# Fused attention and gated feed-forward, one core: how the first batch's keys and queries are loaded, cast and waited for

## The chip, the cores and the metric

The kernel runs on one core of one Trainium2 chip. The metric is device time in microseconds (us) of one execution. The core has a TensorE (PE, with its weight loads listed apart as PEld), a VectorE (DVE), a ScalarE (ACT), a GpSimd (POOL) and a SyncE (SP). SP, ACT and POOL each have a queue from which DMA transfers are issued. In the profile, L185 means line 185 of the kernel.

## The reference

Attention with a squared Relu in place of the softmax, in 8 batches of 12 heads of 448 positions by 64, followed by a gated feed-forward layer on the 3584 rows of 768:

```python
def _attn_ref(q, k, v):
    S = q.shape[2]
    scale = 1.0 / np.sqrt(q.shape[-1])
    scores = scale * np.matmul(q, k.transpose(0, 1, 3, 2))
    attn = np.maximum(scores, 0.0) ** 2 / S
    return np.matmul(attn, v)

def _moe_ref(x, w_gate, w_val, w_out):      # w_gate, w_val: 768 x 1536
    gate = np.maximum(x @ w_gate, 0.0)
    return (gate * (x @ w_val)) @ w_out
```

Inputs and output are float32; the kernel computes in bfloat16 with float32 sums.

## The kernel before

**Layout.** Keys, queries and values of a batch stand in SBUF as `kn`, `qn` and `vn`, `[128, 12, 4, 64]` in bf16: 64 partitions hold four positions each ("lo", positions 0 to 255) and 64 hold three ("hi", 256 to 447). There are two buffers of each. Loading a range of heads of one tensor takes two DMAs, lo and hi (`load_nat`). Pool's queue does this and casts from float32 to bf16 on the way. SP's and ACT's queues cannot cast, so `load_first` brings the first heads of batch 0 as float32 into `kr` and `qr` (tiles that are used for other things much later) and an engine casts them into `kn` and `qn`.

**Order of the loads.** `load_first(2)` brings heads 0 and 1 by SP (lo) and ACT (hi). Then Pool makes the identity matrix and issues, in this order: keys and queries of heads 2 and 3, of heads 4 to 7, of heads 8 to 11 (twelve DMAs), the values of batch 0, the first two chunks of the gate and value weights, batch 1's keys and queries, and the other weights, with `wo` (two halves) last. At most eight of Pool's DMAs are under way at once, in turn.

**Staging.** `first_batch` does batch 0's attention without other work beside it. Heads go in pairs: `transposes` turns a pair's keys and queries by TensorE (matmuls against `ident`, L178) into a PSUM bank, and VectorE copies them out as `kq_sb` (L180). There are 21 tiles of scores, taken in trios: tile 0 to 2 need pair 0, tile 3 to 5 pairs 0 and 1, tile 6 pair 1, tiles 7 and 8 pair 2, and so on. After each trio's scores TensorE transposes the next pair and does a few matmuls on zeros (`idle_matmuls`, on `blank`, two per pair of halves). A tile's scores go to one of three PSUM buffers; ScalarE applies Relu (L185), VectorE squares (L189). From the sixth trio on (tiles `u0` to `u2`, then `w0` to `w2`), `values(qd, c)` multiplies the squared scores with the values, and `cast` brings the result from PSUM into `xT`, the feed-forward layer's input. VectorE does five of these casts (L391) and ScalarE one (L428). Everything is held in program order on each engine (`pin`), so an instruction that waits holds all that follow on its engine.

After that come the units of the feed-forward layer (`gv_unit`: gate and value products, L64 from `mm`; `out_unit`: products with `wo`), mixed with the attention of the next batches. `wo` is first used at about 62 us.

**Lines that the change touches:** `load_first` (L95 to L108), the calls after it in the kernel's body, and `first_batch` with `values`, `cast` and the first `idle_matmuls`. Before, the table of ScalarE's activation functions is loaded (ACT_TABLE_LOAD) ahead of its first activation, the cast of the queries on L108.

Of the kernel before, what the change touches and what calls it, by code (L numbers as in the profile page):

```python
# [10 lines left out]
BF16 = mybir.dt.bfloat16  # L11
AF = mybir.ActivationFunctionType
# [4 lines left out]
def kernel(  # L17
# [15 lines left out]
    nc = tc.nc  # L33

    B, H, S, D = q.shape
# [18 lines left out]
    rpool = ctx.enter_context(tc.tile_pool(name="rpool", bufs=4))  # L54
# [5 lines left out]
    def pin(ins):  # L60
        return tc.keep_in_program_order(ins)
# [4 lines left out]
    def mm2(o, l, r, start, stop):  # L66

        for c in range(2):
            p = slice(c * 64, c * 64 + 64)
            mm(o[p], l[:, p], r, start, stop)  # L70

    NB = 2
    blank = const.tile([128, S], BF16, name="blank")
    pin(nc.vector.memset(blank, 0.0))
    kn_b = [const.tile([128, H, 4, D], BF16, name=f"kn{i}") for i in range(NB)]
    qn_b = [const.tile([128, H, 4, D], BF16, name=f"qn{i}") for i in range(NB)]
# [8 lines left out]
    kr = const.tile([128, 4, d_model], BF16, name="kr")  # L85
    qr = const.tile([128, 4, d_model], BF16, name="qr")

    def make_ident():
        pin(nc.gpsimd.affine_select(out=ident, in_=ident, compare_op=ALU.not_equal, fill=1.0, base=0,
                                    pattern=[[-1, 128]], channel_multiplier=1))  # L90

    def dma_in(o, i):
        pin(nc.gpsimd.dma_start(out=o, in_=i))  # L93

    def load_first(h1):  # L95

        staged = []
        for grp, src in ((kr, k), (qr, q)):
            st = grp.rearrange("p i m -> p (i m)")[:, 0:h1 * 8 * D].bitcast(FP32)
            st = st.rearrange("p (h i d) -> p h i d", i=4, d=D)  # L100
            pin(nc.gpsimd.memset(st[64:128, :, 3, :], 0.0))
            lo = src[0, 0:h1, 0:256, :].rearrange("h (j i) d -> j h i d", i=4)
            hi = src[0, 0:h1, 256:448, :].rearrange("h (j i) d -> j h i d", i=3)
            pin(nc.sync.dma_start(out=st[0:64], in_=lo))
            pin(nc.scalar.dma_start(out=st[64:128, :, 0:3, :], in_=hi))
            staged.append(st)
        pin(nc.vector.tensor_copy(kn_b[0][:, 0:h1], staged[0]))
        pin(nc.scalar.activation(qn_b[0][:, 0:h1], staged[1], AF.Copy))  # L108

    def load_nat(dst, src, b, h0, h1):  # L110
        lo = src[b, h0:h1, 0:256, :].rearrange("h (j i) d -> j h i d", i=4)
        hi = src[b, h0:h1, 256:448, :].rearrange("h (j i) d -> j h i d", i=3)
        dma_in(dst[0:64, h0:h1, :, :], lo)
        dma_in(dst[64:128, h0:h1, 0:3, :], hi)

    def load_qk(b, h0=0, h1=H):
        load_nat(kn_b[b % NB], k, b, h0, h1)
        load_nat(qn_b[b % NB], q, b, h0, h1)

    def load_v(b):  # L120
        load_nat(v_b[b % NB], v, b, 0, H)

    def low_values(b):

        t = v_b[b % NB].rearrange("p (q s h) i d -> p q s h i d", s=2, h=2)
        pin(nc.vector.tensor_copy(t[64:128, :, 1, :, 3, :], t[0:64, :, 1, :, 3, :]))
# [64 lines left out]
    def relu2(src, dst, n):  # L191
        square_part(dst, relu_part(src, n))
# [31 lines left out]
    def av_pair(b, qd, c, attn, ps):  # L224

        p = HALVES[c][1]
        for h2, o in HALVES:
            mm(ps[o, :S], v_b[b % NB][p, 4 * qd + 2 * c + h2, 3, :], attn[p, 6 + h2, :], True, False)
        for i in range(3):
            for h2, o in HALVES:  # L230
                mm(ps[o, :S], v_b[b % NB][:, 4 * qd + 2 * c + h2, i, :], attn[:, 8 * c + 2 * i + h2, :], False, i == 2)

    def bank_tile():
        return psum.tile([128, 512], FP32, name="xT_ps", tag="acc", bufs=2)

    def idle_matmuls(ps, n):

        for _ in range(n):
            mm2(ps[:, :S], blank[:, 0:128], blank, True, True)
# [86 lines left out]
    def gap():  # L326
# [4 lines left out]
        flush()  # L331
        share[2] = i + 1

    load_first(2)
    make_ident()
    load_qk(0, 2, 4)
    load_qk(0, 4, 8)
    load_qk(0, 8, H)
    load_v(0)
    load_gv(0)  # L340
    load_gv(1)
# [14 lines left out]
    def transpose_pair(b, hp, bank=None):  # L356
        kqs[b, hp] = operands(b, hp, bank)

    def attn_of(b, qd):
        if (b, qd) not in attns:  # L360
            attns[b, qd] = atpool.tile([128, 14, S], BF16, name="attn")
        return attns[b, qd]

    def burst(b, tiles):

        todo, begun = [], None
        for qd, kind, c, i in tiles:
            attn = attn_of(b, qd)
            if kind == "pair":
                todo.append(scores(kqs[b, 2 * qd + c], i, attn, 8 * c + 2 * i))  # L370
            elif kind == "last":
                todo.append(scores_last((kqs[b, 2 * qd], kqs[b, 2 * qd + 1]), attn))
            else:
                ps = sc_tile()
                banks = [ps[:, c, :S] for c in range(2)]
                av_last(b, qd, attn, banks)
                begun = (qd, banks, ps[:, :, :S])
        return todo, begun

    def first_batch():  # L380

        def tile_of(n, i):
            return burst(0, [tiles_first[3 * n + i]])[0][0]

        def values(qd, c, on_act=False):
            ps, x = bank_tile(), xT_of[0][:, 2 * qd + c, :]
            av_pair(0, qd, c, attn_of(0, qd), ps)
            return x, ps[:, :S]

        def cast(x, ps):  # L390
            pin(nc.vector.tensor_copy(x, ps))  # L391

        bank = bank_tile()
        idle_matmuls(bank, 14)
        transpose_pair(0, 0, bank)
        bank = bank_tile()
        idle_matmuls(bank, 4)
        for n in range(5):
            t = [tile_of(n, i) for i in range(3)]
            if n == 4:  # L400
                low_values(0)
            transpose_pair(0, n + 1, bank)
            if n < 4:
                bank = bank_tile()
                idle_matmuls(bank, 2)
                for u in t:
                    relu2(*u)
        relu2(*t[0])
        relu2(*t[1])
        u0 = tile_of(5, 0)  # L410
        cast(*values(0, 0))
        relu2(*t[2])
        u1 = tile_of(5, 1)
        cast(*values(0, 1))
        u2 = tile_of(5, 2)
        relu2(*u0)
        relu2(*u1)
        w0 = tile_of(6, 0)
        cast(*values(1, 0))
        relu2(*u2)  # L420
        w1 = tile_of(6, 1)
        cast(*values(1, 1))
        w2 = tile_of(6, 2)
        relu2(*w0)
        relu2(*w1)
        x, ps = values(2, 0)
        relu2(*w2)
        pin(nc.scalar.activation(x, ps, AF.Copy))  # L428
        cast(*values(2, 1))


# [43 lines left out]
    for b in range(B):  # L475
        xT_of[b] = xpool.tile([128, KD, S], BF16, name="xT")
        if b == 0:
            first_batch()
        else:
            batch(b)  # L480
        if b + 1 < B:
            ffn.extend(ffn_units(b))
            if b == 0:
                for _ in range(7):
                    ffn.pop(0)()
                for hp in range(2):
                    midway.append(lambda hp=hp: transpose_pair(1, hp))
                ffn.pop(0)()
# [34 lines left out]
```

## Time and profile before

| | |
|---|---|
| median of 3 runs | 436.48 us (435.64 to 436.99) |
| the profiled execution | 436.3 us, of which 434.5 us are the profile's span |
| TensorE busy | 425.1 us, 98% of the span |
| ScalarE, VectorE, GpSimd busy | 217.6, 210.3 and 50.5 us |
| HBM read, written | 47.19 and 11.01 MB |
| Pool's DMA queue (software_dynamic) | 45152 packets, 23.47 MB |

The span runs from the first instruction to the last; the other 1.8 us of the execution lie around it. A line of the timeline gives start and length in us, the engine, the line of the kernel, the operation, the tiles written and read, how many instructions were merged, and in brackets how long the engine was idle before and what released it. Matmuls are listed with modelled ends, so a busy TensorE is not one at its peak. Idle time of an engine matters only where another engine waits for it.

### The profile page before, as it was taken

The numbers are of one execution on the slowest core, as the hardware profiler recorded it, in microseconds if no ns is written. First come the engines' busy times: TensorE is split into PE (matmuls) and PEld (weight loads), VectorE is DVE, ScalarE is ACT, GpSimd is POOL, SyncE is SP. The second block draws the span as 40 slices with busy tenths as digits, with TensorE's granted clock in tenths as the row PEclk, the third lists the DMA queues.
The fourth block names the chain that finished last, engine by engine and source line by source line (L and its number), as shares of the span: only waits on it lengthen the run. The fifth ranks groups of instructions, "written<-read, shape, count | busy, mean of one in ns | idle before, by whom it ended". The sixth has DMA issues, their size and how long they took to land.

```text
span 434.5 us, 11448 instructions
## 1 busy us (share of the span) xinstructions
PE 425.1 (98%) x5068; PEld 250.2 (58%) x5068; DVE 210.3 (48%) x333; ACT 217.6 (50%) x324; POOL 50.5 (12%) x75
## 2 busy tenths in 40 slices
PE   7899999999999999999999999999999999999996
PEld 3357655655565555655566555655566555565664
DVE  4962784657623665356442675345643454522210
ACT  3952676453554554464554645554545645532221
POOL 8623311100204000300004000010000000000001
PEclk9999999999999999999999999999999999999999
DMA  7999999914699861491616923170413100030014
GB/s 112 174 207 196 200 209 211 227 22 65 105 162 145 122 101 29 91 202 28 110 38 116 187 57 74 38 137 2 99 31 95 53 2 2 10 101 3 2 38 109
DMA packets 78577, 42.45 MB, mean 98 GB/s; under 512 B 48416, under 2 KB 75040, under 8 KB 78528
## 3 DMA queue, kind: packets, MB, share of 16 engines
q0 software_dynamic: 45152, 23.47, 40.6%
q1 hardware_dynamic: 33008, 18.01, 17.6%
q8 instruction: 39, 0.64, 0.6%
q10 hardware_dynamic: 368, 0.25, 0.2%
q14 instruction: 10, 0.08, 0.1%
HBM read 47.19 MB, written 11.01 MB: 134 GB/s over the span
## 4 chain that ended last, share of the span: by engine, by line
PE 84%; DMA 12%; POOL 2%; issue 1%; DVE 0%; POOLq 0%; ACT 0%
PE o_ps L64 25%; PE g_ps L64 23%; PE v_ps L64 22%; PE sc_ps L64 13%; DMA wo<-in_moe_w_out_dram 5%; DMA qn<-in_q_dram 5%; DMA vn<-in_v_dram 2%; POOL kn L93 1%; POOL qn L93 1%; PE kq_ps L178 1%; POOL vn L93 0%; POOL out_dram L303 0%; POOLq L518 0%; DVE qn L81 0%; DVE kn L81 0%
## 5 line engine op out<-in xcount | busy, mean ns | idle before, releaser
L185 ACT ACTIVATE r_sb<-sc_ps 128x896 bf16<-128x896 f32 x168 | 145.0, 931 | 36.7 <-PE sc_ps L64 36.7
L189 DVE TENSOR_TENSOR attn<-r_sb 128x896 bf16<-128x896 bf16 x168 | 103.6, 623 | 92.2 <-ACT r_sb L185 92.1
L64 PE MATMUL g_ps<-xT,wg 128*64 128x448 bf16 x1152 | 126.1, 354 | 0.0
L64 PE MATMUL v_ps<-xT,wv 128*64 128x448 bf16 x1152 | 125.2, 353 | 0.0
L64 PE MATMUL o_ps<-wo,hT 128*64 128x384 bf16 (+1 forms) x1368 | 115.4, 324 | 1.0 <-DMA wo<-in_moe_w_out_dram 1.0
L272 DVE TENSOR_TENSOR hT<-v_ps,g_sb 128x448 bf16<-128x448 f32 x96 | 59.9, 624 | 89.2 <-PE v_ps L64 88.3
L64 PEld LDWEIGHTS <-hT 128*64 128x64 bf16 x1368 | 75.5, 110 | 38.4 <-issue 7.2
L266 ACT ACTIVATE g_sb<-g_ps 128x448 bf16<-128x448 f32 x96 | 52.3, 545 | 89.1 <-PE g_ps L64 89.1
L64 PEld LDWEIGHTS <-wg 128*64 128x64 bf16 x1152 | 63.5, 110 | 49.8 <-issue 13.1
L64 PEld LDWEIGHTS <-wv 128*64 128x64 bf16 x1152 | 66.2, 110 | 41.0
L295 ACT ACTIVATE o_sb<-o_ps 128x384 f32<-128x384 f32 (+1 forms) x57 | 27.9, 489 | 82.1 <-PE o_ps L64 82.1
L64 PE MATMUL sc_ps<-attn,vn 128*64 128x448 bf16 (+1 forms) x336 | 35.1, 354 | 0.0
L93 POOL DMA_DIRECT2D vn<-in_v_dram x16 | 12.1, 771 | 169.2 <-PE sc_ps L64 160.8
L457 DVE CAST xT<-sc_ps 128x896 bf16<-128x896 f32 x21 | 22.9, 1091 | 13.6 <-PE sc_ps L64 13.4
L64 PE MATMUL sc_ps<-qT,kT 64*64 64x448 bf16 x420 | 28.4, 357 | 0.0
L64 PEld LDWEIGHTS <-vn 128*64 128x64 bf16 (+1 forms) x384 | 18.8, 109 | 16.5 <-issue 5.9
L64 PE MATMUL sc_ps<-kq_sb 64*64 64x448 bf16 x252 | 19.0, 360 | 1.6 <-ACT r_sb L185 1.5
L93 POOL DMA_DIRECT2D kn<-in_k_dram x20 | 14.7, 763 | 46.4 <-PE kq_ps L178 44.0
L303 POOL DMA_DIRECT2D out_dram<-o_sb x2 | 1.1, 560 | 146.2 <-ACT o_sb L295 146.2
L64 PEld LDWEIGHTS <-kT 64*64 64x64 bf16 x420 | 9.6, 105 | 14.3 <-issue 11.7
L93 POOL DMA_DIRECT2D qn<-in_q_dram x20 | 14.5, 750 | 6.9 <-DMA vn<-in_v_dram 3.3
L64 PEld LDWEIGHTS <-kq_sb 64*64 64x64 bf16 x252 | 6.4, 105 | 13.0 <-issue 9.7
(33 smaller groups left out, 83.6 us busy)
## 6 DMA issues: line engine op xcount, KB each, us to landing
out_dram<-o_sb SPq DMA_DIRECT2D x54, 192.0 KB, 2.7
vn<-in_v_dram POOLq DMA_DIRECT2D x8, 384.0 KB, 7.0
kn<-in_k_dram POOLq DMA_DIRECT2D x7, 384.0 KB, 10.0
qn<-in_q_dram POOLq DMA_DIRECT2D x7, 384.0 KB, 12.1
vn<-in_v_dram POOLq DMA_DIRECT2D x8, 288.0 KB, 8.1
wo<-in_moe_w_out_dram POOLq DMA_DIRECT2D x2, 1152.0 KB, 20.5
kn<-in_k_dram POOLq DMA_DIRECT2D x7, 288.0 KB, 10.8
qn<-in_q_dram POOLq DMA_DIRECT2D x7, 288.0 KB, 12.9
```

The costliest lines, as they stand in the source:

```text
L64: pin(nc.tensor.matmul(o, lhsT=l, rhs=r, start=start, stop=stop, skip_group_check=True))
L93: pin(nc.gpsimd.dma_start(out=o, in_=i))
L178: pin(nc.tensor.transpose(o, t[:, 2 * hp + h2, i, :], ident))
L185: pin(nc.scalar.activation(r, src, AF.Relu))
L189: pin(nc.vector.tensor_tensor(dst, r, r, ALU.mult))
L266: pin(nc.scalar.activation(g_sb, g_ps, AF.Relu))
L272: pin(nc.vector.tensor_tensor(hT[:, mf, col:col + S], v_ps, g_sb, ALU.mult))
L295: pin(nc.scalar.activation(out=o_sb[:, c0:c1], in_=o_ps, func=AF.Copy, scale=float(out_scale)))
L303: pin(e.dma_start(out=segment_rows(b0, 2 * t + s)[:, m], in_=o_sb[s * 64:s * 64 + 64, m]))
L457: pin(nc.vector.tensor_copy(xT_of[b][:, 2 * qd:2 * qd + 2, :], both))
```

## The change

`load_first` now brings four heads instead of two, in two steps of two heads, keys and queries by SP and ACT (eight DMAs instead of four). ScalarE runs a Relu on the zeros of `blank` right after it has issued its DMAs. Heads 0 and 1 are cast by VectorE, both keys and queries; heads 2 and 3 by ScalarE, both. The identity is made behind these, ahead of Pool's loads as before. Pool then loads heads 4 to 11 of the keys in one pair of DMAs and of the queries in another (four DMAs instead of twelve). The first row of idle matmuls has 17 instead of 14. In `first_batch`, `cast` takes a flag, and the cast of `values(1, 0)` goes to ScalarE, between the Relus of `u1` and `u2`.

```diff
     def load_first(h1):
 
+        nat = (kn_b[0], qn_b[0])
         staged = []
-        for grp, src in ((kr, k), (qr, q)):
+        for grp in (kr, qr):
             st = grp.rearrange("p i m -> p (i m)")[:, 0:h1 * 8 * D].bitcast(FP32)
-            st = st.rearrange("p (h i d) -> p h i d", i=4, d=D)
-            pin(nc.gpsimd.memset(st[64:128, :, 3, :], 0.0))
-            lo = src[0, 0:h1, 0:256, :].rearrange("h (j i) d -> j h i d", i=4)
-            hi = src[0, 0:h1, 256:448, :].rearrange("h (j i) d -> j h i d", i=3)
-            pin(nc.sync.dma_start(out=st[0:64], in_=lo))
-            pin(nc.scalar.dma_start(out=st[64:128, :, 0:3, :], in_=hi))
-            staged.append(st)
-        pin(nc.vector.tensor_copy(kn_b[0][:, 0:h1], staged[0]))
-        pin(nc.scalar.activation(qn_b[0][:, 0:h1], staged[1], AF.Copy))
+            staged.append(st.rearrange("p (h i d) -> p h i d", i=4, d=D))
+            pin(nc.gpsimd.memset(staged[-1][64:128, :, 3, :], 0.0))
+        for h in range(0, h1, 2):
+            for st, src in zip(staged, (k, q)):
+                lo = src[0, h:h + 2, 0:256, :].rearrange("h (j i) d -> j h i d", i=4)
+                hi = src[0, h:h + 2, 256:448, :].rearrange("h (j i) d -> j h i d", i=3)
+                pin(nc.sync.dma_start(out=st[0:64, h:h + 2], in_=lo))
+                pin(nc.scalar.dma_start(out=st[64:128, h:h + 2, 0:3, :], in_=hi))
+
+        pin(nc.scalar.activation(rpool.tile([128, 2, S], BF16, name="r_sb")[:, 0, :], blank, AF.Relu))
+        for h in range(0, h1, 2):
+            for st, t in zip(staged, nat):
+                if h == 0:
+                    pin(nc.vector.tensor_copy(t[:, h:h + 2], st[:, h:h + 2]))
+                else:
+                    pin(nc.scalar.activation(t[:, h:h + 2], st[:, h:h + 2], AF.Copy))
...
-    load_first(2)
+    load_first(4)
     make_ident()
-    load_qk(0, 2, 4)
-    load_qk(0, 4, 8)
-    load_qk(0, 8, H)
+    load_nat(kn_b[0], k, 0, 4, H)
+    load_nat(qn_b[0], q, 0, 4, H)
...
-        def values(qd, c, on_act=False):
+        def values(qd, c):
...
-        def cast(x, ps):
-            pin(nc.vector.tensor_copy(x, ps))
+        def cast(x, ps, on_act=False):
+            if on_act:
+                pin(nc.scalar.activation(x, ps, AF.Copy))
+            else:
+                pin(nc.vector.tensor_copy(x, ps))
 
         bank = bank_tile()
-        idle_matmuls(bank, 14)
+        idle_matmuls(bank, 17)
...
         w0 = tile_of(6, 0)
-        cast(*values(1, 0))
+        cast(*values(1, 0), on_act=True)
         relu2(*u2)
...
-        pin(nc.scalar.activation(x, ps, AF.Copy))
+        cast(x, ps, on_act=True)
```

## The prediction

> **What bounds it now.** I read the page first, then the chain of work that ended last, the waits, the timeline of the first 28 us, and the DMA view in narrow windows of the first 20 us. From the page and the waits:
>
> ```profile
> span 434.5 us, 11448 instructions
> PE 425.1 (98%) x5068; PEld 250.2 (58%) x5068; DVE 210.3 (48%) x333; ACT 217.6 (50%) x324; POOL 50.5 (12%) x75
> PE o_ps L64 <- DMA wo<-in_moe_w_out_dram: 1.0, 1, 1.0
> ```
>
> TensorE is the bound but for 9.4 us: the start, the end, and one wait of 1.0 us for the second half of `wo`. The chain shows what sets the time up to that wait, namely the weights' queue:
>
> ```profile
> 10.98 8.46 DMA vn<-in_v_dram
> 19.73 22.00 DMA qn<-in_q_dram
> 42.63 22.19 DMA wo<-in_moe_w_out_dram
> 64.86 1.17 PE o_ps L64 x12
> ```
>
> So `wo` lands at 42.63 + 22.19 = 64.82, and TensorE, whose last transposes before it end at 63.9 (63.52 and 0.39 in the timeline), has 0.96 us to spare. The new end is 434.5 + max(63.9 + d, 64.82 - e) - 64.82, with d the delay of TensorE's own work and e how much earlier `wo` lands. Nothing that the change touches lies behind 65 us, where TensorE is the bound on its own. Now the start (timeline, 0 to 28 us):
>
> ```profile
> 1.17 4.39 PE L64 MATMUL xT_ps<-blank 128*64 128x448 bf16 x28 [1.17 <-DVE blank L74]
> 3.92 0.61 DVE L107 CAST kn<-kr 128x512 bf16<-128x512 f32 x1 [0.77 <-DMA kr<-in_k_dram]
> 5.06 1.28 ACT L108 ACT_TABLE_LOAD   x1 [5.06 <-DMA qr<-in_q_dram]
> 6.35 0.63 ACT L108 ACTIVATE qn<-qr 128x512 bf16<-128x512 f32 x1
> 7.03 0.41 PE L178 MATMUL xT_ps<-ident,qn 128*64 128x128 bf16 x8 [1.26 <-ACT qn L108]
> ...
> 11.54 0.41 PE L178 MATMUL xT_ps<-ident,kn 128*64 128x128 bf16 x8
> ...
> 11.78 0.39 PE L178 MATMUL xT_ps<-ident,qn 128*64 128x128 bf16 x8
> ```
>
> ```profile
> 8.64 17.11 ACT L185 ACTIVATE r_sb<-sc_ps 128x896 bf16<-128x896 f32 x21 [1.66 <-PE sc_ps L64]
> 26.41 0.54 ACT L428 ACTIVATE xT<-xT_ps 128x448 bf16<-128x448 f32 x1 [0.65 <-PE xT_ps L64]
> ```
>
> ```profile
> 25.70 1.69 DVE L189 TENSOR_TENSOR attn<-r_sb 128x896 bf16<-128x896 bf16 x3
> ...
> 27.43 0.38 PE L64 MATMUL xT_ps<-attn,vn 128*64 128x448 bf16 x2 [0.15 <-DVE attn L189]
> ```
>
> The table load and the query's cast stand between the landed queries (5.06) and the first scores. From 8.64 to 25.75 ScalarE runs 21 Relus with no gap (0.815 us each): the first batch goes at ScalarE's pace, and ends with VectorE's last square (27.39), for which TensorE waits. The third fact is the transposes of heads 4 and 5 at 11.5 to 11.8: their queries (Pool's issues at 6.63 and 7.2, landing 4.4 and 4.3 us later) land at 11.0 and 11.5, so they just make it.
>
> **Part by part: the start.** Queries of heads 0 and 1 are cast on VectorE at 5.06 (0.61, as its cast of the keys), ready at 5.67 instead of 6.98. VectorE has nothing else to do from 4.5 to the copy, so that is free. Three more pairs of idle matmuls cost 3 x 0.21 (five pairs take 4.16 to 5.20), so the keys' transposes begin at 5.82, both sets run on, and the copy follows 0.68 later as in pair 1 (weights 8.89, copy 9.57): copy 6.50 to 7.16, scores 7.21 instead of 8.20. Relu starts 0.44 after them: 7.65 instead of 8.64. On ScalarE's queue two more issues (0.63 and 0.72 in the rows) end near 3.6. Table load (1.28) and the Relu of blank (0.54, the 128x448 row) are done by 5.4, hidden by the wait for data. SP's fourth issue goes at about 3.2 and lands 3.4 later, near 6.6; ScalarE's cast of it (0.63) ends near 7.3, inside 7.65. If these loads are shared out with Pool's and come 0.7 late, it costs 0.35 there. Gain at the first Relu: 1.0, or 0.65 at worst.
>
> **Pool and the queue.** Twelve issues of 0.61 (2.92 to 10.24) become four of about 0.72 (between 0.61 for four heads and 0.82 for twelve), ending at 5.8: `v` and the weights are issued 4.4 us earlier. That does not make them land 4.4 earlier, as the 16 DMA engines are what is short from about 7 us on:
>
> ```profile
> 4.00:5.00 1.00, 1.00 (x10) 0.51 (x8) 0.53 (x1) 0.00 (x0) 1.00 (x3) 1.00 0.62 111
> 5.00:6.00 1.00, 0.78 (x14) 0.44 (x10) 0.00 (x0) 0.94 (x1) 1.00 (x2) 1.00 0.85 91
> 6.00:7.00 1.00, 0.00 (x0) 0.00 (x0) 0.00 (x0) 0.97 (x2) 1.00 (x3) 1.00 0.86 93
> 12.00:13.00 1.00, 0.94 (x20) 0.31 (x15) 0.78 (x2) 1.00 (x2) 1.00 (x2) 1.00 1.39 152
> ```
>
> (Last two columns: DMA share and GB/s.) Only 4 to 7 us have room. I count packets. From 7.9 to 13 us the DMA view has 400 + 357 + 234 + 375 + 352 = 1718, or 337 per us. A load takes one packet per partition and head, and 16 more (SP's and ACT's two each show 288, where 256 are data). Batch 0's keys and queries have 64 x 12 x 4 = 3072: before, 512 + 64 by SP's and ACT's four loads and 2560 + 192 by Pool's twelve. At 337 per us the last of the 2752 is served at about 13.6; it lands at 15.1 (issue at 9.6, 5.5 to landing), and the loads that land from 11 us on all show such a lag of 1.0 to 1.5. After: 1152 by SP and ACT, 2112 by Pool. By 4.3 us 562 are served in either kernel; the other 2702 at 337 per us are through at 12.3. So e = 13.6 - 12.3 = 1.3, and `wo` lands at 63.5. Bounds for e: 0 (the extra written bytes eat it) and 2.1 (375 per us, the best second with Pool's loads in it: through at 11.5).
>
> **The new wait.** Before, heads 4 to 7 had their own loads; now one load holds heads 4 to 11, and TensorE's transposes of heads 4 and 5 wait for all of it, the queries being last. They land at 12.3 plus a lag of 1.1: 13.4. They are wanted at 11.73 - 1.0 = 10.7. Behind the waiting transposes in TensorE's order stand two idle pairs and the scores of tile 6, whose Relu ran at 8.64 + 6 x 0.815 = 13.53. From the queries' first weights (11.73) to those scores (12.48) and 0.44 more is 1.2 us, so that Relu now starts at 14.6: 1.07 later than before, and the whole gain of the start is gone, as ScalarE idles. Bounds: 400 packets per us (the 204 of 2.5 to 3.0 us, from SP and ACT alone) with a lag of 1.0 give 12.05; 295 per us (4096 data packets landed between 7.35 and 19.5 less the first 512) with a lag of 1.5 give 15.0. I take 337, measured over five us of the same packets.
>
> **The cast moved to ScalarE.** It takes 0.62 from VectorE but stands in ScalarE's row after the second Relu of `u`. Before, that Relu ends at 22.5 while the values that it casts are through on TensorE at 23.14, which is TensorE's own chain from 18.51. ScalarE waits 0.7, casts 0.54, and the last four Relus come 1.25 later: 27.0. VectorE no longer lags, and its last square ends 0.62 after that, at 27.64 instead of 27.39. Cost 0.25; as bounds, -0.5 (ScalarE never waits: 25.75 + 0.54 + 0.6 = 26.9) and +0.6.
>
> **Sum.** d = 1.07 + 0.25 = 1.3; TensorE reaches `wo`'s second half at 65.2, and `wo` has landed at 63.5. The spare 0.96 is used up and the rest is lost: 65.2 - 64.82 = 0.4 us. The profiled execution took 436.3 (span 434.5 and 1.8 around it; median of the runs 436.48), so 436.7. With queries between 12.6 and 14.3, its own range is 435.9 to 437.6.
>
> **Rivals.** (1) The loads land in time. If SP's, ACT's and Pool's loads together run above 400 per us and the lag is short, the queries come by 11.3, in time for tile 6 at ScalarE's new pace (7.65 + 4.89 - 1.2), and d = -1.0 + 0.25 = -0.75: TensorE is there at 63.15, `wo` at 63.5 or, with the faster queue, 62.9. The time is 436.3 - 1.3 to 1.7, so 434.6 to 435.0; at 12.0 it is 435.3. For it: the 408 per us at 2.5 us; against it: no stretch with Pool's loads exceeds 375.
> (2) On the other side: TensorE's clock. The first eight idle pairs take 0.375 us each and from 4.16 on 0.2, so the array is at half speed for its first 3.0 us, though the granted clock is written as 1.00 all along. With the queries at 13.4, TensorE does only 0.4 us of transposes between 10.6 and 13.4. If it falls back, a trio of tiles, 1.94 us of TensorE work (shares 0.78, 0.94, 0.66 of 11 to 14 us) under a pace of 2.43, becomes 3.9: 3.0 us of that lose 3.0 - 3.0 x 2.43 / 3.9 = 1.1 us. Time 437.8. It decides from the idle length: the 1.26 us at 5.8 did no harm, 2.8 is untried. The Trainium skill, "TensorE: Matmul & The Clock Gate", part 1 on the clock gate, puts the fall at an idle window of about 3.4 us; by it 2.8 us would be just safe, and a landing after 14 would not.
> (3) The queue is slow: fp32 loads write twice the bytes and crowd Pool's. Queries at 15.0, d = 2.67 + 0.25, time 438.3.
> (4) The part at ScalarE does not do what it says: the table load stays behind the data. The first Relu then starts as before at 8.64, still ahead of 14.6 - 4.9 = 9.7, which the late queries impose, so it is hidden: 436.7. Without that cover it would cost the 1.0 of the start.
>
> **Chances.** Forecast (with 4) 0.48, in time 0.19, clock 0.2, slow queue 0.13. What a measurement tells from no change is 0.3%, 1.3 us. Faster by that: 0.14, three quarters of the first rival. Slower: 0.33, the two slow rivals. Same: 0.53. The range 435.0 to 438.4 leaves out the best of the first rival and the worst of the third.
>
> **What would show it.** First Relu at 7.6 to 8.0; a wait of TensorE (line 178 in this kernel) of over 2 us for DMA `qn` before the third set of query transposes; ScalarE idle for 1.5 us or more before tile 6's Relu; 0.5 to 0.9 us idle before its new cast; no wait for `wo`. Matmuls on blank of 0.37 per pair after 13 us would be the clock. If TensorE doesn't wait for `qn` at all, or still waits for `wo`, the forecast is wrong.

## The result and the profile after

The changed kernel took 437.20 us (median of 16 runs, 436.67 to 438.74) against 436.16 before: ratio 1.0029, 95% interval 1.0017 to 1.0040. A second set beside the experiments gave 1.0019 (1.0009 to 1.0028). It is slower by about 1 us, inside the 0.3% called no change and on its slow side. The profiled execution took 437.25 us, its span and busy times:

```profile
span 435.5 us, 11463 instructions
PE 427.8 (98%) x5074; PEld 251.6 (58%) x5074; DVE 210.1 (48%) x333; ACT 219.2 (50%) x327; POOL 46.4 (11%) x67
```

Its first 29 us (timeline; line 116 holds ScalarE's cast of heads 2 and 3, 186 the transposes, 193 the Relu):

```profile
1.17 5.85 PE L64 MATMUL xT_ps<-blank 128*64 128x448 bf16 x34 [1.17 <-DVE blank L74]
...
3.48 1.28 ACT L110 ACT_TABLE_LOAD   x1 [3.48 <-issue]
...
5.12 0.45 DVE L114 CAST qn<-qr 128x512 bf16<-128x512 f32 x1 [0.76 <-DMA qr<-in_q_dram]
...
6.85 0.39 PE L186 MATMUL xT_ps<-ident,kn 128*64 128x128 bf16 x8
...
8.56 0.63 ACT L116 ACTIVATE qn<-qr 128x512 bf16<-128x512 f32 x1 [2.27 <-DMA qr<-in_q_dram]
...
9.10 4.94 ACT L193 ACTIVATE r_sb<-sc_ps 128x896 bf16<-128x896 f32 x6
...
13.06 0.64 PE L186 MATMUL xT_ps<-ident,qn 128*64 128x128 bf16 x8 [0.67 <-DMA qn<-in_q_dram]
...
15.02 9.02 ACT L193 ACTIVATE r_sb<-sc_ps 128x896 bf16<-128x896 f32 x11 [0.98 <-PE sc_ps L64]
```

The table load and the first queries' cast are out of the way, as the change says. But the 17 idle pairs ran on until the keys' transposes began at 6.85 us: 13 of them took 0.375 us each, where before eight did, so the clock rose just after 6.03 instead of just after 4.16. The queries of heads 2 and 3, by SP and ACT, were cast only at 8.56, and ScalarE's first Relu, queued behind that cast, came at 9.10 instead of 8.64. Then the third set of query transposes waited for the merged load, and tile 6's Relu came at 15.02 instead of 13.53. The stretches around that wait, with columns length, busy time (and instructions) of PE, PEld, DVE, ACT and POOL, granted clock, DMA share and GB/s:

```profile
12.00:13.00 1.00, 0.39 (x12) 0.23 (x8) 0.27 (x1) 1.00 (x2) 0.76 (x1) 0.99 1.47 195
13.00:14.00 1.00, 0.94 (x12) 0.64 (x12) 0.27 (x1) 1.00 (x2) 0.75 (x1) 0.50 1.49 202
14.00:15.00 1.00, 1.00 (x12) 0.39 (x12) 1.00 (x3) 0.04 (x1) 0.00 (x0) 0.50 1.58 190
15.00:16.00 1.00, 1.00 (x16) 0.36 (x10) 0.99 (x2) 0.98 (x2) 0.00 (x0) 0.50 1.40 204
16.00:17.00 1.00, 1.00 (x22) 0.64 (x19) 0.34 (x1) 1.00 (x2) 0.70 (x1) 0.80 1.26 205
```

The granted clock fell to half at 13.0, and was back at 16.4. At `wo` TensorE no longer waits (the first line below ends at 65.82, and the next row follows without an idle time):

```profile
65.43 0.39 PE L186 MATMUL kq_ps<-ident,qn 128*64 128x128 bf16 x8
...
65.65 1.14 PE L64 MATMUL o_ps<-wo,hT 128*64 128x384 bf16 x12
```

Its transposes end 1.9 later than the 63.9 of before, and the second half of `wo` had landed at 62.6 (issue at 40.21, 22.4 to landing). 65.82 - 64.86 is the 1.0 us by which the span grew.

### The profile page after: what moved, and what is told of

It is laid out like the page before. It is cut to its first block, busy times and chain, and to the rows that moved or that the text cites. A ratio compares the mean times of both kernels' runs of the same rounds, so it can differ in the third digit from the quotient of the medians.

```text
span 435.5 us, 11463 instructions
## 1 busy us (share of the span) xinstructions
PE 427.8 (98%) x5074; PEld 251.6 (58%) x5074; DVE 210.1 (48%) x333; ACT 219.2 (50%) x327; POOL 46.4 (11%) x67
## 4 chain that ended last, share of the span: by engine, by line
PE 93%; DVE 2%; DMA 2%; POOL 1%; ACT 1%; issue 1%; POOLq 0%; ACTq 0%
PE g_ps L64 26%; PE o_ps L64 25%; PE v_ps L64 25%; PE sc_ps L64 15%; DMA qn<-in_q_dram 2%; DVE attn L197 1%; PE kq_ps L186 1%; ACT r_sb L193 1%; DVE kq_sb L188 0%; POOL kn L93 0%; PE xT_ps L186 0%; PE xT_ps L64 0%; DVE xT L401 0%; POOL qn L93 0%; POOLq L528 0%
## 5 line engine op out<-in xcount | busy, mean ns | idle before, releaser
L64 PEld LDWEIGHTS <-vn 128*64 128x64 bf16 (+1 forms) x384 | 18.9, 109 | 16.4 <-issue 6.0
L93 POOL DMA_DIRECT2D kn<-in_k_dram x16 | 12.3, 776 | 51.3 <-PE kq_ps L186 47.7
L93 POOL DMA_DIRECT2D qn<-in_q_dram x16 | 12.0, 766 | 5.3 <-DMA vn<-in_v_dram 5.3
```

What stands on the lines that cost most here:

```text
L64: pin(nc.tensor.matmul(o, lhsT=l, rhs=r, start=start, stop=stop, skip_group_check=True))
```

## The experiments

All were run in three sets, each beside runs of the kernel before on the same chip; five rounds each. Medians of before: 436.52 (e1 to e4), 436.53 (e5 to e8), 436.63 (e9 to e11).

**e1_split**, the changed kernel with Pool's loads split again:

```diff
-    load_nat(kn_b[0], k, 0, 4, H)
-    load_nat(qn_b[0], q, 0, 4, H)
+    load_qk(0, 4, 8)
+    load_qk(0, 8, H)
```

> The changed kernel with Pool's loads of heads 4 to 11 split again into heads 4 to 7 and 8 to 11 (keys and queries of each). Theory (the late queries of heads 4 to 11, with the clock's fall in their wait, are the loss): the queries of heads 4 to 7 land 1.5 us or more before 12.9, TensorE's wait of 2 us before the third set of query transposes shrinks below 1 us, the granted clock does not fall to 0.5 between 13 and 16 us, and the time comes to 435.3 to 436.3, ratio to before 0.998 to 1.000. Rival (the cast on ScalarE and the three more idle pairs are the loss): the wait shrinks but the time stays within 0.3 us of 437.2, ratio about 1.002.

435.98 us (435.61 to 436.41), ratio 0.9989 (0.9980 to 0.9998). TensorE's wait for `qn` is gone altogether and the clock stays at 1.00. ScalarE's timeline in it:

```profile
8.16 13.85 ACT L193 ACTIVATE r_sb<-sc_ps 128x896 bf16<-128x896 f32 x17
22.75 0.54 ACT L399 ACTIVATE xT<-xT_ps 128x448 bf16<-128x448 f32 x1 [0.74 <-PE xT_ps L64]
23.19 3.34 ACT L193 ACTIVATE r_sb<-sc_ps 128x896 bf16<-128x896 f32 x4
```

Seventeen Relus without a gap, begun 0.5 us earlier than before. The new cast makes ScalarE wait 0.74 and work 0.54. Splitting these loads alone turns the change from a loss to a small gain. It does not show that the wait for `qn` was the whole loss, though: in this profile the queries of heads 2 and 3 were also cast earlier (7.62, against 8.56 in the changed kernel), and the first Relu came 0.94 earlier than there.

**e7_merge**, the kernel before with the merged loads alone:

```diff
-    load_qk(0, 4, 8)
-    load_qk(0, 8, H)
+    load_qk(0, 4, H)
```

> The kernel before with one part of the change alone: Pool loads heads 4 to 11 in one pair of DMAs for keys and one for queries; heads 0 to 3 as before. Theory (merging the loads is what makes TensorE wait): the third set of query transposes waits until about 14.5 instead of 11.78, tile 6's Relu starts 2 us late, the spare 0.96 us at wo takes part of it, and the time rises by 0.8 to 1.8 us, ratio 1.002 to 1.004. Rival (the competition of SP's and ACT's loads with Pool's is what makes it late, and merging is harmless without it): within 0.3 us of before.

438.60 us, ratio 1.0045 (1.0032 to 1.0059): 2 us of loss from the merging alone, a little more than expected. Its transposes waited 3 us, the rival falls, and the clock fell too, for twice as long. The transposes' line in its timeline, and stretches of it:

```profile
14.99 0.64 PE L178 MATMUL xT_ps<-ident,qn 128*64 128x128 bf16 x8 [2.97 <-DMA qn<-in_q_dram]
```

```profile
13.00:14.00 1.00, 0.00 (x0) 0.00 (x0) 0.00 (x0) 0.50 (x1) 0.12 (x1) 0.74 1.31 159
14.00:15.00 1.00, 0.01 (x2) 0.04 (x3) 0.00 (x0) 0.00 (x0) 0.76 (x1) 0.50 1.46 198
...
18.00:20.00 2.00, 2.00 (x24) 0.99 (x24) 1.33 (x3) 1.53 (x3) 0.75 (x1) 0.50 1.25 211
```

**e10_merge_fill**, e7_merge with matmuls on zeros in the wait:

```diff
+            if n == 1:
+                idle_matmuls(bank, 12)
             transpose_pair(0, n + 1, bank)
```

> The kernel before with heads 4 to 11 in merged loads, as e7_merge, and 12 pairs of idle matmuls (2.4 us) in the wait of 3 us that this made. Theory (the wait makes the clock fall, and the fall is worth about 1.1 us on top of the wait): granted clock 1.0 after 13 us, and 0.8 to 1.5 us below e7_merge, ratio 1.001 to 1.003. Rival (ScalarE paces the first batch, the clock costs nothing): the clock stays up and the time is that of e7_merge, ratio 1.004 to 1.005.

437.63 us, ratio 1.0022 (1.0011 to 1.0032). The wait is still there, but the clock is 1.00 throughout its profile's first 20 us, and the time is 1.0 us below e7_merge (medians; the intervals of the ratios touch only at 1.0032):

```profile
15.43 0.41 PE L178 MATMUL xT_ps<-ident,qn 128*64 128x128 bf16 x8 [1.29 <-DMA qn<-in_q_dram]
```

In the two profiles the first products with `wg` begin at 31.65 (e7) and 30.72 (e10), although e10's queries landed later (15.30 against 14.85). So the fall of the clock by itself is worth about 1 us, and the wait the other 1 us of the merging's 2.

**e3_fill**, the same filling with six pairs in the changed kernel (`idle_matmuls(bank, 6)` at that place).

> The changed kernel with six more pairs of idle matmuls ahead of the third set of transposes, inside TensorE's wait for the queries. Theory (the clock falls because of the wait): no stretch at a granted clock of 0.5 after the start, the first batch ends about 1 us earlier than in the changed kernel, the runs scatter less, and the time is 436.4 to 436.9. Rival (the wait alone costs it, the clock costs nothing as ScalarE paces): same time as the changed kernel within 0.3 us, 437.0 to 437.5, clock back at 1.0.

438.48 us, ratio 1.0044 (1.0030 to 1.0058), on five runs: both expectations missed. In its profile the clock did stay at 1.0 after the start, but the queries of heads 2 and 3 were cast only at 9.04, TensorE reached the filling at 12.46, and it ran until 13.6, although the queries had landed at 12.78: without the filling TensorE would have been ready for them at about 12.9 (12.46 and 0.41 for the keys' transposes), with no wait left to fill. That is the profile of the fastest of the five runs. The run that is the median, 438.48, has a span of 435.5 and 3.0 us outside it, where the other four have 1.7 to 1.9. So why the median is 1.2 above the changed kernel's stays open; that a fill costs time where there is no wait to fill fits it. On the clock's price this run settles nothing.

**e5_after**, the changed kernel again.

> The changed kernel unchanged, beside the others on one chip, for a second profile of it. Theory (two loads come late in turn: the queries of heads 2 and 3 by SP and ACT, cast on ScalarE, and the queries of heads 4 to 11 by Pool): ratio to before 1.002 to 1.004; in the profile one or both waits are there again, the first Relu later than 8.64 and tile 6's Relu later than 14.2, whether the granted clock falls or not. Rival (the profile's fall of the clock is the loss): where the clock stays at 1.0 the time is that of before within 0.3 us.

437.30 us, ratio 1.0019 (1.0009 to 1.0028). In this profile the clock stayed up, the first Relu came at 9.38, the wait for `qn` was 0.51 us, tile 6's Relu followed in the row without a gap, and the transposes at `wo` ended at 65.07, 1.17 later than before. Of that the late first Relu is 0.74, and the other 0.4 lies behind it, where the new cast stands; the wait for `qn` added nothing.

```profile
8.85 0.63 ACT L116 ACTIVATE qn<-qr 128x512 bf16<-128x512 f32 x1 [0.98 <-DMA qr<-in_q_dram]
9.38 13.98 ACT L193 ACTIVATE r_sb<-sc_ps 128x896 bf16<-128x896 f32 x17
```

One fall of 3.4 us to half lowers the mean granted clock of the span by 0.004. Its runs with a mean granted clock of 0.998 or more have a median of 437.09 and the four others 437.70; in the first set of 16 runs, seven such have 436.82 and nine others 438.02. So, if the lower means are such falls, the loss without them is 0.6 to 0.7 us, and they add 0.6 to 1.2. The rival falls.

**e11_act_cast**, the kernel before with the cast of `values(1, 0)` on ScalarE alone (`cast` with its flag, as in the change).

> The kernel before with one part of the change alone: the cast of values(1, 0) on ScalarE. Theory (it ends the first batch 0.25 to 0.4 us later, but TensorE has 0.96 us to spare before the second half of wo): the first products with wg begin 0.2 to 0.5 us later than 27.62, the wait for wo shrinks by as much, and the time stays within 0.3 us of before. Rival (VectorE is the bound, the move is a gain): the products begin earlier.

436.26 us, ratio 0.9998 (0.9990 to 1.0007): no change, as expected. From the first Relu to the last two matmuls with the values it is 27.79 - 8.68 = 19.11 us; before, 27.43 - 8.64 = 18.79. The cast costs 0.32 us, and the spare time at `wo` hides it. TensorE now waits longer for the last square (timeline of this kernel; 0.15 before):

```profile
27.79 0.38 PE L64 MATMUL xT_ps<-attn,vn 128*64 128x448 bf16 x2 [0.43 <-DVE attn L189]
```

**e2_dve_cast**, the changed kernel with the cast back: `cast(*values(1, 0))`.

> The changed kernel with the cast of values(1, 0) back on VectorE. Theory (the cast costs 0.25): ScalarE's 0.8 us of waiting and 0.54 us of cast go, VectorE gets 0.62 more, and the time is 0.2 to 0.5 us below the changed kernel's 437.2, so 436.7 to 437.0. Rival (VectorE is the bound there and the move is a gain): 0.3 to 0.6 us above it, 437.5 or more.

437.19 us, ratio 1.0013 (1.0003 to 1.0024). The expected 436.7 to 437.0 was missed: the median is that of the changed kernel (437.20 and 437.30), its ratio is lower than 1.0019 and 1.0029, and the intervals overlap, so the cast's cost is not settled by this run. But its profile is the plainest case of the late start. The granted clock is 1.00 in all of it and the wait for `qn` 0.19 us, and yet its span is 435.5, as long as the changed kernel's. SP's fourth load landed at 9.95:

```profile
10.05 0.63 ACT L116 ACTIVATE qn<-qr 128x512 bf16<-128x512 f32 x1 [2.72 <-DMA qr<-in_q_dram]
10.59 17.09 ACT L193 ACTIVATE r_sb<-sc_ps 128x896 bf16<-128x896 f32 x21
```

The first Relu is 1.95 later than before, and the first products with `wg` (29.55 against 27.62) are 1.93 later. By the scores (8.56 and 0.44) it could have begun at 9.00: 1.6 of the delay is the late queries of heads 2 and 3, the rest the long idle pairs.

**e6_split_dve**, e1_split with the cast back as in e2.

> Pool's loads split as in e1_split and the cast of values(1, 0) back on VectorE. Theory (the cast costs 0.25): 0.2 to 0.5 us below e1_split, so 0.9975 to 0.9985 of before, with the last square of the first batch 0.2 to 0.4 us earlier. Rival (a wash, or VectorE is the bound): the ratio is that of e1_split, 0.9989, or above.

435.58 us, ratio 0.9978 (0.9969 to 0.9987), 0.4 us below e1_split. First Relu to last two matmuls: 27.64 - 8.87 = 18.77 against e1's 27.24 - 8.16 = 19.08. Neither profile has a wait at `wo`, so the 0.31 us can show in the time, and the medians fit that; the intervals of the two ratios overlap between 0.9980 and 0.9987.

**e4_start**, the kernel before with the blank Relu behind ScalarE's DMA issues and the first queries cast by VectorE:

```diff
+        pin(nc.scalar.activation(rpool.tile([128, 2, S], BF16, name="r_sb")[:, 0, :], blank, AF.Relu))
         pin(nc.vector.tensor_copy(kn_b[0][:, 0:h1], staged[0]))
-        pin(nc.scalar.activation(qn_b[0][:, 0:h1], staged[1], AF.Copy))
+        pin(nc.vector.tensor_copy(qn_b[0][:, 0:h1], staged[1]))
```

> The kernel before with two parts of the change's start alone: ScalarE's Relu of blank right after its DMA issues, and the queries of heads 0 and 1 cast by VectorE; 14 idle pairs and all loads as before. Theory (the table load and the cast stood in the way): scores begin 0.8 to 1.2 us earlier than 8.20, TensorE's wait for the second half of wo grows from 1.0 to about 2 us since wo does not land earlier, and the time stays within 0.3 us of before, 435.9 to 436.4. Rival (the early start is worth what it saves): 435.2 or less.

436.66 us, ratio 1.0002 (0.9992 to 1.0012). The median is 0.1 from before, and the rival falls. The first step was smaller than expected: scores at 7.85 instead of 8.20, as the idle pairs were long here too; and TensorE then waited 0.3 for `qn` and 0.6 for `vn`, so that the first products with `wg` began at 27.94, 0.3 later than before. The wait for `wo` did not grow to 2 us (waits of this kernel):

```profile
PE o_ps L64 <- DMA wo<-in_moe_w_out_dram: 1.1, 1, 1.1
```

What was gained at the start was worth nothing here, with the loads in their old order.

**e8_split_idle12**, e1_split with `idle_matmuls(bank, 12)` at the start.

> Pool's loads split as in e1_split and 12 pairs of idle matmuls at the start instead of 17. Theory (how long the idle pairs take hangs on when the clock rises; at half speed 17 pairs end after the queries of heads 0 and 1 are cast, near 5.6): the scores begin at 7.0 to 7.3 whenever the clock rises, at best 0.3 us is gained on e1_split and the runs scatter as little or less. Rival (the clock rises later with fewer matmuls, or falls): 0.3 us or more above e1_split.

435.86 us, ratio 0.9981 (0.9970 to 0.9991): 0.1 below e1_split, which these intervals can't tell from nothing; the expected gain was 0.3 at best. Scores at 7.26, but the first Relu at 9.12, behind the cast of the queries of heads 2 and 3: in this profile those bound it, not the idle pairs.

**e9_best**, e6_split_dve with 12 idle pairs, to see what adds up.

> The changed kernel with Pool's loads split, the cast of values(1, 0) on VectorE and 12 idle pairs: what the runs so far speak for, put together. Theory (the cast's 0.4 us and the split's 1.3 us add, the idle pairs' count is worth 0.1 to 0.2): ratio 0.997 to 0.998, at or a little below e6_split_dve. Rival (with 12 pairs the clock or the late queries of heads 2 and 3 bind): 0.3 us or more above e6_split_dve, ratio over 0.9985.

435.43 us (435.15 to 435.74), ratio 0.9969 (0.9956 to 0.9981): the fastest, 1.2 us below the kernel before and 1.8 below the changed one's median (437.2, from another set). It is 0.15 below e6, so the idle pairs' part is not shown by itself.

## Why the prediction held, step by step

**Where the time is set.** The end followed max(63.9 + d, 64.82 - e) as written: with d = 1.9 the new end came out at 65.82, and TensorE did not wait for `wo`. The runs show both sides of that maximum. In e4 and e11 d was 0.3 and 0.4, the end went by `wo`, and `wo` alone moved it: it landed 0.46 later in e4 (65.28) and 0.47 earlier in e11 (64.35), and the spans are 0.5 longer and 0.5 shorter than before. In the eight profiles with the new start (after, e1, e2, e3, e5, e6, e8, e9) TensorE is the later one: the span differs from that of before by d less 0.96 to 1.0 us, with d read from the first products with `wg` (-0.19 in e1, 0.09 in e9, 1.16 in e5, 1.93 in e2).

**The merged load makes TensorE wait for heads that it needs six tiles later.** The wait is there, and e7 shows that merging alone makes it and costs time. The queries landed at 12.92 (forecast 13.4). The size of the wait was wrong: 0.67 and 0.51 us in the two profiles, not over 2, since TensorE itself was ready for them at 12.4 and 12.7 instead of the forecast 10.7. In e7, where it was ready at 12.0 and nothing else had changed, the wait was 3 us. In the changed kernel it was a small part of the loss: e2 and e5 lose theirs without it.

**The start.** This is the term that failed: a gain of 1.0 was forecast, "0.65 at worst", and the first Relu came 0.46 and 0.74 later than before. Two durations were mis-sized. The idle pairs were priced at 0.21 us, the row after the clock had risen, but when it rises is not fixed: 13 slow pairs in one profile where the profile of before had eight. And the loads of heads 2 and 3 by SP and ACT: 3.4 us to landing was taken from SP's second load, and 4.4 to 6.8 us were measured for its fourth, with three loads of SP ahead of it and Pool's beside it (5.3 and 5.6 in the changed kernel). The bound of 0.7 for that was too small by over 1 us there. The cast of those queries is what the first Relu stood behind: the scores at 8.22 and 0.44 would have given 8.66. So in that profile the long idle pairs ate the gain of 1.0, and the late cast added the 0.4 behind it.

**Tile 6's Relu**, 14.6 forecast, was at 15.02, but of its 1.5 us against before 0.46 are the late start, 0.1 the queries (12.92 and 1.2 is 14.1), and 0.9 the clock, at which the transposes and scores behind the queries took 2.0 instead of 1.2.

**How much was luck.** The time lies in the stated range, and two of the five signs were there: 0.82 and 0.74 us idle before the new cast, and no wait for `wo`. Three were not: the first Relu at 9.10 and 9.38 instead of 7.6 to 8.0, waits for `qn` of 0.67 and 0.51 instead of over 2, and ScalarE idle for 0.98 and not at all, instead of 1.5 or more, before tile 6's Relu. A start that was 1.5 to 1.7 us later than forecast took the place of most of the wait that had been forecast, so the sum came out near d = 1.3 (1.17 in e5, 1.9 with the clock's fall). That the two errors nearly cancel is luck; what held is the delay d against the spare time at `wo`.

**The clock.** Told as a rival at 0.2 with 1.1 us; a lower mean clock shows in 9 of 16 and in 4 of 12 executions, and e7 against e10 gives 1.0 us. The forecast 436.7 is near the 436.82 of the runs without it; the median of all, 437.2, mixes both. What was said to decide it was wrong: not a wait of 2.8 us. It fell after a wait of 0.67, in a stretch (9.6 to 13.0) where TensorE was busy 2.28 of 3.4 us. But how busy that stretch is does not decide it either: in the same stretch the clock stayed up with 2.90 in the kernel before, with 2.56 in e5, and with only 1.96 in e2, where TensorE had also waited longer, 1.07 us (the same stretch of the changed kernel and of e2):

```profile
9.60:13.00 3.40, 2.28 (x28) 0.70 (x22) 2.38 (x4) 3.40 (x5) 2.40 (x3) 1.00 1.49 192
9.60:13.00 3.40, 1.96 (x24) 0.69 (x21) 1.76 (x3) 2.95 (x5) 1.64 (x2) 1.00 1.40 170
```

What decides it stays open. The rule cited from the Trainium skill, "TensorE: Matmul & The Clock Gate", part 1, is an idle window of about 3.4 us. The trace disagrees: here no wait in the stretch before the fall was over 0.67 us, and in e7 the clock fell 1.5 us into the wait (12.0 to 13.5). Its length of window agrees: the half clock lasted 3.4 us here (13.0 to 16.4) and 6.8 in e7 (13.5 to 20.3).

**The cast on ScalarE**, 0.25, measured 0.32 and 0.31. The mechanism is as told: 0.74 to 0.82 us of waiting for the values and 0.54 of work.

**`wo`**, e = 1.3 forecast, measured 64.82 - 62.6 = 2.2; no harm, since TensorE was later still. The slow queue of the third rival was partly true between 4.3 and 7.9 us (976 packets, 271 per us, not 337) and made up later.

What stays open: whether the size of Pool's loads makes SP's and ACT's late. The cast that waits for them began at 8.6, 10.1, 9.0 and 8.9 in the four profiles with merged loads (after, e2, e3, e5), and at 7.6, 8.3, 8.6 and 8.2 in the four with split ones (e1, e6, e8, e9): that points to it, but these are single profiles that scatter by over 1 us. No run holds Pool's loads back, so SP's own three loads ahead of the fourth remain a rival.

## What to carry to other kernels

A transfer that is merged to save issues makes its first user wait for its last byte: look at when the first part is wanted before counting the issues saved (in e7 eight issues became four, and the kernel lost 2 us, about half of it by the clock that fell in the wait). A gain ahead of a wait for another queue is worth only as much as that queue moves too. A load that is moved to another queue should be priced with all that is issued ahead of it and beside it (5.3 us to landing, where 3.4 had been read from an earlier load). Matmuls on zeros that keep TensorE's clock up should be counted in time, at the slow price, and not longer than the data that they bridge.

## What the hardware showed

The clock at the start rose just after 4.16 us in one profile, just after 6.03 in another and just after 6.77 in a third (e5), with the same matmuls up to there. Later it fell to half after a stretch of 3.4 us with TensorE busy for 2.28 and no wait over 0.67 us, and in another profile it stayed up with 1.96 in the same stretch and a wait of 1.07; when it fell in the wait of e7, that cost about 1 us. And with loads of three queues under way, SP's fourth load of 128 KB took 4.4 to 6.8 us to land, where its second, in the kernel before, took 3.4.
